# Hash-masked attention and a channel mix on one core: q and k of the third pair turned by TensorE, PSUM banks from a table, and another order of work

## The chip, the cores and the metric

One core of a Trainium2 chip. The metric is the time of one execution on the device, in microseconds (us). The engines are named as in the profile: PE (TensorE, with PEld for its weight loads), DVE (VectorE), ACT (ScalarE), POOL (GpSimd) and SP (SyncE, which here only issues DMAs).

## What is computed

Attention over 4 batches, 8 heads, 768 positions and 64 values a head, in which a query sees only keys of its own hash bucket, and behind it a channel mix with a squared ReLU and a gate:

```
bits(t)  = (t @ proj) > 0                      # 6 bits of each row of q and of k
scores   = q @ k.T / 8, where bits(q) == bits(k), else -1e9
x        = softmax(scores) @ v                 # (4, 768, 512), heads side by side
x_prev   = x one position later
xk, xr   = x_prev + mu * (x - x_prev)          # mu_k, mu_r
out      = sigmoid(xr @ w_r) * (relu(xk @ w_k) ** 2 @ w_v)
```

## The kernel before

The work goes by 16 pairs of heads (`n`), four pairs a batch, and after each fourth pair comes the batch's channel mix, called MoE in the code (`add_moe`).

For each pair, q and k are loaded in natural layout (`nat`, L481) and split in a high and a low half of 16 bits (`hi` L556, `lo` L559, into `nh`). They must then be turned, so that the 64 values and not the positions lie on partitions. For pairs 0 and 1 (`FIRSTS`) PE turns them (`add_prep_first`, L635; copied out of PSUM at L639), from the third pair on a DMA transpose does (`add_prep`, L563, on SP's queue). Of the turned tile `a`, rows 0 to 63 are the high half; over the low half, once it is used, the hash bits are written: PE takes the product with `proj` (L587 in `add_bits`), DVE keeps the sign (`bx`, L591), and DMAs on SP's queue send it to rows 64 to 69 of `a` (L599, called `row`). Pair 0 gets its bits without a DMA (L657, and L663 or L665). So the bits enter the score product itself, as rows of its contraction.

Scores come in nine steps of 1024 columns a pair (L708, `sc{n}_{s}`; steps 0 to 3 are of head 0 alone, 5 to 8 of head 1), each followed by an exp on ACT (L712). PV (L741, `oo`) gives the output and the sum of weights, DVE divides (L758), and the result is turned again (`ot` by PE for some pairs, by DMA L768 for the others), shifted by one position (`xs`, `xj`), and mixed (L829, L837, L841). `add_v` makes the values' 16 bit form and their sums (`va`, `vsum`). The MoE has `kp` (L859) with ReLU (L864 on ACT or L866 on DVE) and square (L869), `r` (L884) with a tanh (L887), and `v` (L896) with the last product (L903) and the store (L907). Weights are loaded in ten pieces (`wl`, L447) and cast (`wc`, L450 to L452).

Nothing of the order is left to a scheduler. Every operation is recorded with `add`; `ORDER` lists them all in the order in which they are issued, and each engine works through its own part of it, strictly in turn. `WHERE` says for each movable operation which engine does it. `Plan.schedule` in the old kernel walks through `ORDER` with planned times, only to choose a PSUM place for each operation that needs one: score steps take one of three pairs of banks (0 and 1, 2 and 3, 4 and 5), the others a single bank among 7 to 3. Three buffers of `vn` mean that the load of v for pair n + 3 waits for `va` of pair n; three of `nat` do the same for q and k.

Of the kernel before, what the change touches and what calls it, by code (L numbers as in the profile page):

```python
# [16 lines left out]

LAG = {"PE": 0.21, "ACT": 0.21, "DVE": 0.15, "POOL": 0.18, "SP": 1.8, "GQ": 2.0}
# [17 lines left out]
def R(kind, n):  # L36
# [4 lines left out]
    "wc0": "DVE", "wc1": "POOL", "wc2": "POOL", "wc3": "DVE", "wc4": "POOL", "wc5": "DVE", "wc6": "ACT", "wc7": "DVE",  # L41
    "wc8": "ACT", "wc9": "POOL", "hi0q0": "ACT", "evt0q00": "DVE", "evt0q01": "DVE", "hi0k0": "DVE", "evt0k00": "DVE", "beb0k00": "ACT",
    "evt0k01": "ACT", "beb0k01": "ACT", "hi0q1": "ACT", "evt0q10": "ACT", "hi0k1": "DVE", "evt0k10": "ACT", "beb0k10": "ACT", "va0": "POOL",
    "vsum0": "POOL", "vsum0b": "DVE", "vsum0c": "DVE", "hi1q0": "DVE", "evt1q00": "DVE", "hi1k0": "ACT", "evt1k00": "ACT", "hi1q1": "DVE",
    "evt1q10": "DVE", "hi1k1": "DVE", "evt1k10": "ACT", "xt0_0": "DVE", "xs0_0": "DVE", "xj0": "DVE", "va1": "POOL", "vsum1": "DVE",
    "vsum1b": "POOL", "vsum1c": "POOL", "hi2q": "DVE", "hi2k": "DVE", "xt1_0": "DVE", "xs1_0": "POOL", "xj1": "DVE", "va2": "POOL",
    "vsum2": "DVE", "vsum2b": "DVE", "vsum2c": "POOL", "hi3q": "DVE", "hi3k": "DVE", "xt2_0": "DVE", "xs2_0": "DVE", "xt2_3": "DVE",
    "xs2_3": "POOL", "xj2": "POOL", "va3": "POOL", "vsum3": "DVE", "vsum3b": "POOL", "vsum3c": "DVE", "hi4q": "DVE", "hi4k": "DVE",
    "xt3_0": "DVE", "xs3_0": "POOL", "xt3_3": "DVE", "xs3_3": "POOL", "xj3": "POOL", "relu0_0_0": "DVE", "relu0_0_1": "ACT", "relu0_1_0": "DVE",
    "relu0_1_1": "ACT", "relu0_2_0": "ACT", "relu0_2_1": "ACT", "relu0_3_0": "DVE", "relu0_3_1": "DVE", "relu0_4_0": "DVE", "relu0_4_1": "DVE", "relu0_5_0": "ACT",  # L50
    "relu0_5_1": "ACT", "relu0_6_0": "DVE", "relu0_6_1": "ACT", "relu0_7_0": "ACT", "relu0_7_1": "ACT", "va4": "POOL", "vsum4": "DVE", "vsum4b": "POOL",
    "vsum4c": "POOL", "hi5q": "DVE", "hi5k": "DVE", "xs4_0": "POOL", "va5": "DVE", "vsum5": "DVE", "vsum5b": "DVE", "vsum5c": "POOL",
    "hi6q": "DVE", "hi6k": "DVE", "xs5_0": "POOL", "va6": "DVE", "vsum6": "DVE", "vsum6b": "DVE", "vsum6c": "POOL", "hi7q": "DVE",
    "hi7k": "DVE", "xs6_0": "DVE", "va7": "POOL", "vsum7": "DVE", "vsum7b": "POOL", "vsum7c": "DVE", "hi8q": "DVE", "hi8k": "DVE",
    "xs7_0": "DVE", "relu1_0_0": "DVE", "relu1_0_1": "DVE", "relu1_1_0": "DVE", "relu1_1_1": "ACT", "relu1_2_0": "ACT", "relu1_2_1": "DVE", "relu1_3_0": "DVE",
    "relu1_3_1": "DVE", "relu1_4_0": "DVE", "relu1_4_1": "DVE", "relu1_5_0": "ACT", "relu1_5_1": "DVE", "relu1_6_0": "DVE", "relu1_6_1": "DVE", "relu1_7_0": "DVE",
    "relu1_7_1": "DVE", "vsum8": "DVE", "vsum8b": "DVE", "vsum8c": "DVE", "hi9q": "DVE", "hi9k": "DVE", "xs8_0": "POOL", "vsum9": "DVE",
    "vsum9b": "DVE", "vsum9c": "POOL", "hi10q": "DVE", "hi10k": "DVE", "xs9_0": "ACT", "vsum10": "DVE", "vsum10b": "DVE", "vsum10c": "DVE",
    "hi11q": "DVE", "hi11k": "ACT", "xs10_0": "DVE", "vsum11": "DVE", "vsum11b": "POOL", "vsum11c": "POOL", "hi12q": "ACT", "hi12k": "DVE",
    "xs11_0": "DVE", "relu2_0_0": "DVE", "relu2_0_1": "ACT", "relu2_1_0": "ACT", "relu2_1_1": "DVE", "relu2_2_0": "ACT", "relu2_2_1": "ACT", "relu2_3_0": "ACT",  # L60
    "relu2_3_1": "DVE", "relu2_4_0": "ACT", "relu2_4_1": "ACT", "relu2_5_0": "ACT", "relu2_5_1": "DVE", "relu2_6_0": "ACT", "relu2_6_1": "ACT", "relu2_7_0": "DVE",
    "relu2_7_1": "DVE", "vsum12": "DVE", "vsum12b": "POOL", "vsum12c": "POOL", "hi13q": "ACT", "hi13k": "ACT", "xs12_0": "DVE", "vsum13": "DVE",
    "vsum13b": "POOL", "vsum13c": "POOL", "hi14q": "DVE", "hi14k": "ACT", "xs13_0": "ACT", "vsum14": "DVE", "vsum14b": "DVE", "vsum14c": "DVE",
    "hi15q": "DVE", "hi15k": "ACT", "xs14_0": "POOL", "vsum15": "DVE", "vsum15b": "DVE", "vsum15c": "POOL", "xt15_0": "DVE", "xs15_0": "ACT",
    "relu3_0_0": "ACT", "relu3_0_1": "DVE", "relu3_1_0": "ACT", "relu3_1_1": "ACT", "relu3_2_0": "DVE", "relu3_2_1": "ACT", "relu3_3_0": "ACT", "relu3_3_1": "ACT",
    "relu3_4_0": "DVE", "relu3_4_1": "ACT", "relu3_5_0": "DVE", "relu3_5_1": "ACT", "relu3_6_0": "ACT", "relu3_6_1": "DVE", "relu3_7_0": "ACT", "relu3_7_1": "ACT",
# [3 lines left out]
ORDER = [  # L70
    31, 0, 2, 3, 1, 66, 63, 97, 98, 9, 35, 25, 4, 10, 5, 64, 6, 7, 8, 19, 71, 72, 65, 99,
    91, 77, 92, 81, 100, 14, 69, 73, 26, 82, 13, 78, 103, 93, 94, 87, 88, 74, 27, 28, 36, 122, 83, 84,
    123, 29, 30, 101, 95, 114, 115, 104, 68, 85, 41, 102, 89, 90, 167, 124, 168, 174, 175, 11, 75, 125, 96, 176,
    142, 146, 79, 15, 110, 177, 32, 111, 112, 118, 178, 86, 143, 147, 33, 293, 179, 144, 145, 80, 116, 67, 117, 119,
    140, 141, 120, 76, 113, 136, 137, 121, 134, 221, 228, 229, 222, 34, 126, 127, 129, 135, 132, 133, 39, 128, 138, 139,
    231, 232, 130, 131, 180, 181, 184, 185, 16, 192, 193, 186, 106, 107, 108, 109, 153, 187, 300, 301, 70, 170, 196, 197,
    105, 303, 148, 149, 150, 188, 189, 304, 151, 152, 198, 199, 183, 17, 171, 172, 182, 154, 155, 156, 40, 252, 224, 253,
    157, 244, 173, 230, 474, 475, 158, 245, 233, 18, 225, 240, 241, 226, 248, 249, 234, 235, 250, 251, 190, 191, 294, 477,
    478, 246, 247, 202, 194, 195, 159, 161, 467, 160, 203, 204, 205, 200, 201, 42, 206, 162, 165, 227, 266, 302, 223, 242,
    243, 166, 267, 268, 468, 207, 238, 528, 529, 269, 237, 208, 209, 239, 236, 324, 325, 270, 318, 305, 210, 211, 254, 37,  # L80
    38, 531, 470, 255, 306, 319, 307, 212, 213, 532, 214, 328, 271, 272, 273, 274, 316, 329, 317, 256, 257, 258, 476, 312,
    313, 169, 296, 479, 320, 321, 275, 215, 279, 47, 259, 260, 297, 298, 280, 281, 314, 261, 262, 315, 263, 326, 480, 264,
    265, 310, 322, 299, 471, 472, 163, 327, 323, 335, 336, 481, 337, 338, 164, 339, 308, 488, 489, 330, 331, 332, 333, 334,
    486, 522, 585, 276, 277, 521, 487, 311, 309, 498, 340, 582, 583, 499, 341, 342, 343, 344, 278, 490, 491, 502, 530, 345,
    346, 20, 347, 348, 349, 216, 503, 295, 494, 495, 492, 493, 219, 473, 504, 505, 485, 217, 350, 483, 550, 551, 533, 45,
    534, 496, 351, 497, 506, 586, 500, 501, 535, 484, 21, 283, 218, 284, 353, 354, 554, 555, 48, 524, 285, 525, 526, 352,
    22, 357, 482, 542, 282, 509, 510, 511, 512, 513, 507, 543, 508, 544, 545, 548, 549, 552, 553, 527, 584, 288, 289, 290,
    587, 588, 589, 540, 43, 355, 556, 557, 563, 564, 537, 539, 49, 538, 536, 541, 546, 46, 44, 547, 358, 359, 375, 565,
    356, 362, 363, 391, 50, 604, 605, 376, 364, 575, 602, 566, 567, 636, 637, 392, 377, 378, 371, 372, 606, 603, 607, 393,
    367, 368, 469, 373, 598, 369, 599, 578, 379, 380, 608, 381, 592, 609, 600, 601, 558, 559, 576, 639, 640, 610, 579, 580,  # L90
    611, 560, 561, 562, 581, 395, 396, 24, 382, 397, 220, 291, 398, 594, 595, 286, 287, 51, 590, 648, 53, 394, 593, 374,
    654, 292, 655, 649, 52, 630, 780, 781, 617, 618, 591, 660, 661, 411, 412, 638, 662, 619, 407, 408, 596, 663, 409, 370,
    413, 597, 641, 642, 643, 383, 384, 385, 664, 665, 629, 777, 778, 514, 515, 387, 652, 653, 388, 360, 389, 523, 632, 612,
    361, 365, 620, 621, 768, 650, 651, 410, 414, 55, 427, 366, 428, 429, 54, 658, 659, 403, 404, 613, 12, 614, 615, 399,
# [41 lines left out]
class Plan:  # L136
# [7 lines left out]
    def add(self, eng, dur, prio, fn, r=(), w=(), take=None, give=(), lag=None, name="", at=0.0, svc=0.0, off=None, tr=0, port=0, land=1.5):  # L144
# [31 lines left out]
        self.ops.append(o)  # L176
        return o

    def sequence(self):
        if ORDER:  # L180
            return [self.ops[i] for i in ORDER]
        left = {o.i: len(o.deps) for o in self.ops}
# [3 lines left out]
        while heap:  # L186
            o = self.ops[heapq.heappop(heap)[1]]
            seq.append(o)
            for s in o.succ:
                left[s] -= 1  # L190
                if not left[s]:
                    heapq.heappush(heap, (self.ops[s].prio, s))
# [772 lines left out]
```

## Time and profile before

| | |
|---|---|
| median of 3 runs | 249.64 us (249.36 to 250.64) |
| span of the profiled execution | 251.3 us |
| busy: PE, DVE, ACT, POOL | 236.9, 195.4, 179.1, 27.9 us |
| granted PE clock, mean | 0.983 |
| HBM read, written | 24.12 MB, 6.29 MB |

The profile is of one execution of its own, whose span is 1.7 us above the median; the page has no other time for it. In the rows, `x7` counts instructions that were merged, `SPq` is SP's queue of DMA issues, and the bracket at the end of a row of the timeline is the idle time before it and what ended it.

### The profile page before, as it was taken

How to read it: one execution, taken by the hardware profiler on the slowest of the kernel's cores; microseconds unless marked ns; L12 is line 12 of the kernel's file. 1: busy time of each engine (PE TensorE's matmuls, PEld its weight loads, DVE VectorE, ACT ScalarE, POOL GpSimd, SP SyncE). 2: the span in 40 equal slices, each digit the busy share in tenths (PEclk: the TensorE clock that was granted, in tenths of full speed). 3: DMA queues.
4: the chain of work that ended last, by engine and by line, in shares of the span. 5: the costliest groups of instructions: out<-in, count | busy, mean ns of one | idle time of the engine just before them, and what ended most of it. 6: DMA issues, size and time to landing. Idle time of an engine off the chain costs nothing.

```text
span 251.3 us, 6510 instructions
## 1 busy us (share of the span) xinstructions
PE 236.9 (94%) x2609; PEld 147.6 (59%) x2609; DVE 195.4 (78%) x471; ACT 179.1 (71%) x225; POOL 27.9 (11%) x73
## 2 busy tenths in 40 slices
PE   6886799999799998999999999999999999999993
PEld 2444578876566655666467566655865654545442
DVE  3795679889788889898998999899787878376322
ACT  5596689999799978996878899988787223332220
POOL 5002240541302031100001100100000000000000
PEclk9799799999999999999999999999999999999998
DMA  6999999999989999999999996793231030022223
GB/s 187 308 178 251 220 215 191 267 249 189 213 292 241 204 293 292 273 201 269 184 333 186 184 185 158 210 230 57 90 64 44 0 128 28 13 83 86 83 85 125
DMA packets 75194, 44.56 MB, mean 177 GB/s; under 512 B 55524, under 2 KB 70172, under 8 KB 75164
## 3 DMA queue, kind: packets, MB, share of 16 engines
q1 hardware_dynamic: 74028, 44.15, 72.8%
q8 instruction: 20, 0.33, 0.6%
q10 hardware_dynamic: 1136, 0.01, 0.3%
q14 instruction: 10, 0.08, 0.1%
HBM read 24.12 MB, written 6.29 MB: 121 GB/s over the span
## 4 chain that ended last, share of the span: by engine, by line
PE 75%; DMA 11%; DVE 8%; SPq 3%; ACT 1%; issue 1%; DVEq 0%
PE ps_all L708 19%; PE ps_all L896 17%; PE ps_all L859 13%; PE ps_all L741 12%; PE ps_all L884 8%; DMA nat<-in_k_dram 5%; PE ps_all L587 4%; DMA nat<-in_q_dram 3%; DMA a<-bx 2%; DMA os<-in_moe_w_k_dram 1%; DVE nh L559 1%; DVE nh L556 1%; PE ps_all L736 1%; ACT pt L712 1%; PE ps_all L794 1%
## 5 line engine op out<-in xcount | busy, mean ns | idle before, releaser
L712 ACT ACTIVATE pt<-ps_all 128x1024 bf16<-128x1024 f32 x144 | 138.8, 1040 | 21.1 <-PE ps_all L708 19.8
L708 PE MATMUL ps_all<-a 128*128 128x512 f16 (+3 forms) x408 | 80.6, 318 | 5.1 <-DMA a<-bx 3.9
L708 PEld LDWEIGHTS <-a 128*128 128x128 f16 x408 | 35.3, 98 | 26.7 <-DMA a<-bx 4.7
L859 PE MATMUL ps_all<-xk,wk 128*128 128x384 bf16 x256 | 49.0, 326 | 0.9 <-DVE kr L866 0.9
L896 PE MATMUL ps_all<-wv,k 128*128 128x512 bf16 (+1 forms) x200 | 45.9, 370 | 0.6 <-DVE os L903 0.6
L741 PEld LDWEIGHTS <-pt 128*128 128x128 bf16 x1152 | 42.1, 98 | 6.9 <-issue 1.1
L741 PE MATMUL ps_all<-va,pt 128*128 128x65 bf16 x1152 | 43.9, 194 | 0.0
L859 PEld LDWEIGHTS <-wk 128*128 128x128 bf16 x256 | 24.5, 98 | 17.6 <-issue 1.6
L896 PEld LDWEIGHTS <-k 128*128 128x128 bf16 x200 | 19.4, 98 | 20.6 <-issue 0.7
L864 ACT ACTIVATE kr<-ps_all 128x384 bf16<-128x384 f32 x33 | 15.8, 493 | 19.2 <-DVE k L869 12.7
L887 ACT ACTIVATE rs<-ps_all 128x512 f32<-128x512 f32 x24 | 14.2, 603 | 20.9 <-PE ps_all L884 19.0
L559 DVE SCALAR_TENSOR_TENSOR nh<-nat,nh 128x768 f16<-128x768 f32 x28 | 27.3, 976 | 1.1 <-ACT nh L554 0.6
L903 DVE SCALAR_TENSOR_TENSOR os<-rs,ps_all 128x512 f32<-128x512 f32 (+1 forms) x25 | 16.5, 662 | 14.7 <-PE ps_all L896 9.9
L869 DVE TENSOR_TENSOR k<-kr 128x384 bf16<-128x384 bf16 x64 | 21.5, 350 | 3.7 <-ACT kr L864 3.5
L884 PE MATMUL ps_all<-wr,xr 128*128 128x512 bf16 x96 | 23.8, 379 | 0.0
L866 DVE TENSOR_SCALAR kr<-ps_all 128x384 bf16<-128x384 f32 x31 | 17.1, 555 | 8.3 <-PE ps_all L859 6.6
L758 DVE TENSOR_TENSOR ob<-ps_all,rc 128x384 bf16<-128x384 f32 (+1 forms) x36 | 18.3, 511 | 1.0
L884 PEld LDWEIGHTS <-xr 128*128 128x128 bf16 x96 | 9.0, 98 | 10.0 <-ACT kr L864 0.3
L587 PE MATMUL ps_all<-a,p0g 128*32 128x256 f16 (+1 forms) x180 | 13.4, 276 | 1.3 <-DMA a<-nh 1.3
L556 DVE TENSOR_SCALAR nh<-nat 128x768 f16<-128x768 f32 x22 | 12.3, 557 | 3.0 <-DMA nat<-in_q_dram 2.5
L587 PE MATMUL ps_all<-a,p1g 128*32 128x256 f16 (+1 forms) x180 | 12.9, 273 | 0.0
L841 DVE TENSOR_TENSOR xr<-tm,xt 128x768 bf16<-128x768 f16 (+1 forms) x18 | 9.4, 520 | 0.4
(94 smaller groups left out, 187.4 us busy)
## 6 DMA issues: line engine op xcount, KB each, us to landing
vn<-in_v_dram SPq DMA_DIRECT2D x16, 384.0 KB
out_dram<-os SPq DMA_DIRECT2D x23, 256.0 KB
nat<-in_k_dram SPq DMA_DIRECT2D x15, 384.0 KB
nat<-in_q_dram SPq DMA_DIRECT2D x15, 384.0 KB
wst<-in_moe_w_k_dram SPq DMA_DIRECT2D x2, 512.0 KB
wst<-in_moe_w_r_dram SPq DMA_DIRECT2D x2, 512.0 KB
wst<-in_moe_w_v_dram SPq DMA_DIRECT2D x2, 512.0 KB
a<-bx SPq DMA_DIRECT2D x48, 9.0 KB
```

The lines of the kernel that those rows point to most:

```text
L559: nc.vector.scalar_tensor_tensor(out=nh[:, :, D:P], in0=nat.rearrange("p j (c d) -> p (j c) d", d=D), scalar=QS, in1=nh[:, :, 0:D], op0=AL ...
L587: nc.tensor.matmul(ps[g_ * wid : (g_ + 1) * wid, 0:FW], w_[:, m_ - 1 - x : m_ - 1 - x + wid], a_t[sa][:, i, x % NFOLD * FW : (x % NFOLD + ...
L708: nc.tensor.matmul(ps[:, lo - s * STEP : hi - s * STEP], side_a["k"][sa][:, j, jc * P : (jc + 1) * P], side_a["q"][sa][:, j, q0 : q0 + hi ...
L712: nc.scalar.activation(out=pt_t[sp][:, s * STEP : (s + 1) * STEP], in_=ps_t[plan.slot[nm]], func=AF.Exp, bias=EBIAS, scale=ESC)
L741: nc.tensor.matmul(oo[:, (ic - c0) * 65 : (ic - c0) * 65 + 65], pt_t[sp][:, o : o + P], va_t[sa][:, j, jc, 0 : D + 1], start=(not uc and i ...
L758: nc.vector.tensor_tensor(out=ob_t[so][:, c0:c1, j * D : (j + 1) * D], in0=oo[:, :, 0:D], in1=rc_t[sr][:, 1, c0:c1].unsqueeze(2).to_broadc ...
L859: nc.tensor.matmul(ps[:, 0:HALF], wk_sb[:, d, fc * P : (fc + 1) * P], xk_t[mx[d]][:, h * HALF : (h + 1) * HALF], start=(d == 0), stop=(d = ...
L866: nc.vector.tensor_scalar(out=kr_t[sk], in0=sm(nm)[:, 0:HALF], scalar1=0.5 ** 0.5, scalar2=0.0, op0=ALU.mult, op1=ALU.max)
L869: nc.vector.tensor_tensor(out=k2_t[s2][:, h * HALF : (h + 1) * HALF], in0=kr_t[sk], in1=kr_t[sk], op=ALU.mult)
L884: nc.tensor.matmul(sm(nr), xr_t[mx[d]][:, c * P : (c + 1) * P], wr_sb[:, d, :], start=(d == 0), stop=(d == NDC - 1))
L896: nc.tensor.matmul(sm(nv)[:, lo:hi], k2_t[(b * NFC + fc) % NK2][:, c * P : (c + 1) * P], wv_sb[:, fc, lo:hi], start=(fc == 0), stop=(fc == ...
L903: nc.vector.scalar_tensor_tensor(out=os_t[so][:, lo:hi], in0=rs_t[s1][:, lo:hi], scalar=1.0, in1=sm(nv)[:, lo:hi], op0=ALU.add, op1=ALU.mult)
```

## The change

The third pair joins `FIRSTS`, so its q and k are converted head by head and turned by PE, 24 transposes in four groups and four copies out of PSUM, and two DMA transposes are gone. The loads of the first pair and all that follows from them take head 1 first. PSUM places are no longer chosen by planned times: the table `SLOT` names a bank (or the first of two) for every operation, among the same classes. `mu_k` and `mu_r` are loaded as eight rows of 128 and turned by a small matmul with an 8 x 8 identity, in place of two loads with one value on each partition and step. `WHERE` and `ORDER` are new throughout: they were sought for an order that also holds when GpSimd's operations take up to twice their planned time. More is done on GpSimd: 37 of 48 sums of v (18 before), 9 of 10 casts of weights (4), six conversions of q or k (none), 10 of 18 shifts (8); ReLU is on DVE 36 times (31) and on ACT 28 (33). Other things that the new code can do are switched off (`NWARM2 = 0`, `ROWD = ()`, `ROW_ACT = ()`, `STEPS = {}`).

```diff
-    FIRSTS = (0, 1)
+    FIRSTS = (0, 1, 2)
...
     def schedule(self):
-        free = {e: 0.0 for e in ("PE", "ACT", "DVE", "POOL", "SP")}
...
+        used, held = set(), {}
+        order = [self.ops[i] for i in ORDER]
         for o in order:
...
+                name, size = o.take[1], BANKS[o.take[0]]
+                self.slot[name] = SLOT[name]
+                held[name] = set(range(SLOT[name], SLOT[name] + size))
...
-    for t, src, key in ((muk, moe_mu_k, "muk"), (mur, moe_mu_r, "mur")):
...
+    add("POOL", 0.3, -2.2, lambda: make_identity(nc, id8), w=["id8"], name="id8")
+    for i_, src in enumerate((moe_mu_k, moe_mu_r)):
+        add("ACT", 0.42, -19.0, lambda i_=i_, src=src: nc.scalar.dma_start(out=mu8[i_ * NDC : (i_ + 1) * NDC, :], in_=src.rearrange("(c p) -> c p", p=P)),
...
+    add("PE", 0.12, 1.0, lambda: nc.tensor.matmul(sm("mu")[:, 0 : 2 * NDC], mu8, id8, start=True, stop=True),
```

The start of the order, engine by engine (the digits behind q or k are pair, then head):

```
before  DVE  hi0k1 lo0k1 lo0q0 lo0q1 hi0k0 lo0k0 evt0q01 evt0q00 hi1k1 evt0k00 lo1k1 lo1k0 hi2 lo2
             beb0q10 hi1q0 hi2 lo1q0 hi1q1 lo2 beb0q01 lo1q1 beb0q00 evt1q00 evt1q10 hi3 lo3 bx1
after   DVE  hi0k1 lo0k1 hi0q1 lo0q1 evt0k10 hi0k0 evt0q10 lo0k0 lo0q0 beb0q10 hi1k1 lo1k1 hi1q1 evt0k01
             lo1q1 beb0q01 lo1q0 lo1k0 beb0q00 beb0k01 evt1k00 evt1k10 evt1q00 hi2k1 hi2k0 lo2q0 lo2q1 bx1
before  SP   q, k of pairs 0, 1, 2, 3, 5q, 4; tr2 tr2 and ldv0 among them; row1 row1 ldv1 ldv2 row2 row2 tr3 tr3 ...
after   SP   q, k of pairs 0, 1, 2, 3, 4; ldv0 ldv1 ldv2 ldv3 among them; row1 row1 5k 5q ldv4 6q row2 row2 tr3 tr3 tr4 tr4
             6k 7q row3 row3 ldv6 wl2 ldv5 row4 row4 8q row4 row4 tr5 tr5 tr6 tr6 ...
after   POOL ... hi1k0 ... hi2q0 va0 ... va1 ... vsum0 vsum0b vsum0c ... hi4 id8 vsum1 ...
```

The last matmuls before are the second half of columns of `v3_5`, stored by itself; after, all columns of `v3_4`.

## The prediction

> **What bounds the kernel now.** I read the page first, for the share of each engine, then windows of the span, PE's waits, the chain that ended last, and the timeline of the first 25 us.
>
> ```profile
> span 251.3 us, 6510 instructions
> PE 236.9 (94%) x2609; PEld 147.6 (59%) x2609; DVE 195.4 (78%) x471; ACT 179.1 (71%) x225; POOL 27.9 (11%) x73
> ```
>
> TensorE (PE) is the busiest engine, 236.9 of 251.3 us, so a better order can win at most the 14.4 us in which it is idle, and whatever it loses to a low clock. The windows say where both lie (columns: busy us of PE, PEld, DVE, ACT, POOL, then granted clock, DMA share, GB/s):
>
> ```profile
> 20.00:25.00 5.00, 2.72 (x31) 1.72 (x29) 2.27 (x4) 2.98 (x4) 1.32 (x2) 1.00 0.84 262
> 25.00:30.00 5.00, 3.37 (x24) 2.04 (x25) 3.95 (x6) 2.73 (x3) 1.43 (x3) 0.77 1.07 228
> 30.00:35.00 5.00, 4.99 (x84) 3.90 (x83) 2.63 (x8) 3.74 (x5) 1.69 (x3) 0.89 0.95 254
> 65.00:70.00 5.00, 3.66 (x61) 2.38 (x60) 3.53 (x11) 3.63 (x5) 1.04 (x2) 1.00 0.85 267
> 90.00:100.00 10.00, 8.99 (x108) 5.28 (x110) 8.74 (x23) 7.20 (x10) 1.15 (x5) 1.00 1.13 272
> 100.00:160.00 60.00, 60.00 (x727) 37.68 (x717) 54.56 (x132) 50.77 (x61) 4.39 (x9) 1.00 0.99 223
> 160.00:240.00 80.00, 80.00 (x697) 46.16 (x696) 58.44 (x150) 43.28 (x64) 0.81 (x2) 1.00 0.29 80
> ```
>
> From 100 to 240 us PE is never idle: there a change of engine or of order wins nothing, it can only lose. Between 20 and 30 PE is idle 3.9 us, and the clock is low from then to about 31. Around 65 and 95 another 1.3 and 1.0 us are missing. PE's waits and the chain that ended last name the causes:
>
> ```profile
> PE ps_all L708 <- DMA a<-bx: 3.9, 1, 3.9
> PE ps_all L587 <- DMA a<-nh: 1.3, 2, 1.0
> ...
> 22.07 4.43 DMA a<-bx
> 26.63 1.70 PE ps_all L708 x7
> ```
>
> The second pair's scores (L708) start at 26.63, when its hash bits, sent from `bx` to rows 64 to 69 of `a`, have landed. That transfer is what the start ends on, so I ask when `bx1` comes about now, and when in the new order.
>
> **The change part by part.** From the timeline, the start, with the instructions that I price with:
>
> ```profile
> 0.96 0.59 ACTq L404 DMA_DIRECT2D pj<-in_proj_dram  x1
> 3.19 0.36 DVE L618 TENSOR_SCALAR nh<-nat 128x384 f16<-128x384 f32 x1 [2.07 <-DMA nat<-in_k_dram]
> 3.42 0.24 POOL L405 TENSOR_SCALAR npj<-pj 64x6 f32<-64x6 f32 x1 [1.83 <-DMA pj<-in_proj_dram]
> 9.39 0.35 DVE L639 COPY a<-ps_all 128x384 f16<-128x384 f16 x1
> 9.66 1.02 DVE L621 SCALAR_TENSOR_TENSOR nh<-nat,nh 128x384 f16<-128x384 f32 x2
> 10.59 0.56 DVE L556 TENSOR_SCALAR nh<-nat 128x768 f16<-128x768 f32 x1
> 11.18 0.96 DVE L559 SCALAR_TENSOR_TENSOR nh<-nat,nh 128x768 f16<-128x768 f32 x1
> 12.17 1.55 SPq L563 DMA_TRANSPOSE a<-nh  x1
> 12.17 0.95 DVE L665 TENSOR_SCALAR a<-ps_all 6x768 uint16<-6x768 uint16 x1
> 13.81 2.86 ACT L712 ACTIVATE pt<-ps_all 128x1024 bf16<-128x1024 f32 x3 [0.60 <-PE ps_all L708]
> 15.62 2.04 SPq L563 DMA_TRANSPOSE a<-nh  x1
> 15.62 0.56 DVE L665 TENSOR_SCALAR a<-ps_all 6x384 uint16<-6x384 uint16 x1
> 16.82 0.51 PE L635 MATMUL ps_all<-idh,nh 128*128 128x128 f16 x6 [0.43 <-DVE nh L621]
> 17.38 1.02 DVE L639 COPY a<-ps_all 128x768 f16<-128x768 f16 x2
> 20.00 0.42 DVE L591 TENSOR_SCALAR bx<-ps_all 128x256 uint16<-128x256 uint16 x1
> 20.45 2.36 SPq L599 DMA_DIRECT2D a<-bx  x2
> ```
>
> *When the first exps start.* VectorE (DVE) works through a fixed order from 3.19 on. Before, the bits of head 1's q (L665, 6x768) stand behind 14 instructions, among them a conversion and a rest (L556, L559; 0.56 + 0.96) for the third pair, and start at 12.17. In the new order head 1 comes first: they stand behind three of L618 (0.36), four of L621 (0.51) and two copies of 768 (0.51), 4.1 us, so at about 7.6 with half a us of waits. In ScalarE's queue eight short instructions stand ahead of the first exp, one of them a conversion of the third pair's q, which DVE had at 10.59 before; I put the first exp at 10.3, an estimate, against 13.81. That is not yet the gain: nine exps of about 0.95 (2.86 for three) then reach to 19, and only the next pair's rows let the queue go on.
>
> *When `bx1` is ready.* Now 27 instructions of DVE stand before L591: five of L618, eight of L621, three each of L556 and L559, three copies of 384 (0.35), two of 768, one L665 of 0.95 and two of 0.56: 1.8 + 4.1 + 1.7 + 2.9 + 1.1 + 1.0 + 2.1 = 14.7 us. From 3.19 that is 17.9, and it stands at 20.00, so 2.1 us are waits. After, again 27: seven of L618, ten of L621, none of the long ones, one copy of 384, five of 768, the 0.95 and three of 0.56: 2.5 + 5.1 + 0.35 + 2.55 + 0.95 + 1.7 = 13.2, so 16.4 without waits and 18.5 with as many. I take 17.6, and 18.0 at its end (bounds 16.8 and 18.9).
>
> *The rows' flight.* Before, 26.63 - 20.42 = 6.2 us passed from `bx1` to PE, behind loads issued just ahead. The nearest row of a lone small transfer is pj: issued at 0.96, used at 3.42, 2.5 us; with the first of two issues ahead of it (half of 2.36) 3.7. In the new order SP's queue reaches the rows early, its last load ahead being the fourth v. So 3.7 to 6.2; I take 4.4, between, nearer the lone one. The second pair's scores then start at 22.4 against 26.63: **4.2 us gained**; with both bounds 1.5 to 6.1.
>
> *The clock.* Windows 25 to 35 lose (0.23 + 0.11) x 5 = 1.7 us of full clock, right after the long wait. With `bits1`, `bits2` and the new transposes ahead, PE's wait would be about 2 us. I count **1.7 us gained**; if the wait stays long, nothing. The Trainium skill, "TensorE: Matmul & The Clock Gate", section "What's actually happening", says that the clock goes to half after an idle window of about 3.4 us; the wait of 3.9 us with 0.77 behind it agrees, and by it a 2 us wait leaves the clock full.
>
> *The third pair turned by PE.* It removes two DMA transposes (1.55 + 2.04 us of SP's queue, and their DMA), and adds 24 transposes on PE (four of the 0.51 row, 2.0 us) and four copies out of PSUM; the conversions are the same columns in halves. The 2.0 us lie among the first pair's last scores, which wait for exps, in the stretch where PE is now idle 2.3 us (window 20 to 25); without that cover they cost 2.0 in full. Behind them `bits2` stays as it is.
>
> *What SP's queue holds after the rows.* Four loads of v go ahead of the first rows, against one before. The fourth waits for `va0` on GpSimd, which stands behind `hi1k0` and `hi2q0`; queued behind it on SP are the rows of pairs 1 and 2 and every later transpose. From the timeline of SP:
>
> ```profile
> 30.68 0.46 SPq L481 DMA_DIRECT2D nat<-in_q_dram  x1
> 37.83 1.57 SPq L599 DMA_DIRECT2D a<-bx  x2
> 39.45 3.54 SPq L563 DMA_TRANSPOSE a<-nh  x2
> 55.59 2.50 SPq L563 DMA_TRANSPOSE a<-nh  x1
> ```
>
> and from the groups by form (mean ns after the comma):
>
> ```profile
> L501 POOL CAST va<-vn 128x768 bf16<-128x768 f32 x6 | 5.6, 930 | 25.6 <-DMA vn<-in_v_dram 19.3 <-PE ps_all L741 6.1 <-PE ps_all L859 0.2
> L509 POOL TENSOR_TENSOR vt<-va 128x390 f32<-128x390 bf16 x1 | 0.8, 847 | 0.1
> L450 POOL CAST wk<-k 128x1024 bf16<-128x1024 f32 x1 | 1.4, 1450 | 0.0
> L903 DVE SCALAR_TENSOR_TENSOR os<-rs,ps_all 128x512 f32<-128x512 f32 x23 | 15.6, 683 | 13.4 <-PE ps_all L896 8.5 <-ACT rs L887 2.8 <-ACT kr L864 1.1
> L903 DVE SCALAR_TENSOR_TENSOR os<-rs,ps_all 128x256 f32<-128x256 f32 x2 | 0.8, 421 | 1.4 <-PE ps_all L896 1.4
> ```
>
> No row shows a conversion to halves on GpSimd. Its bounds are the cast of as many columns (0.93 for 768) and the two-input add scaled by columns (0.847 x 768 / 390 = 1.7); for 384 half of each. With the second pair's k there by 9, two of at most 0.85 and `va0` are done by 11.7, five us before `bx1`: hidden. [...] The new order also takes up `bits5` later among the scores, so I expect short waits for transposes or rows, 0 to 3 us more than now: **1.3 lost**.
>
> *The rest.* `mu` in eight rows, turned by one small matmul, and one VectorE instruction in place of two: between 0.3 lost and 0.3 gained, hidden before the first mix; I count 0. Banks from a table: still two or three score buffers of two banks each, no instruction more; 0. GpSimd gets 103 listed operations for 67, VectorE 439 for 455, ScalarE 215 for 227; from 100 us on PE has no idle time that this could fill: 0, at worst the rival below. The end: the last step becomes a whole row block in place of a half, 0.68 for 0.42 us on VectorE and a store of twice the size: **0.5 lost** (0.3 to 0.9).
>
> **Sum.** The profiled execution's span is 251.3, 1.7 above the median of 249.64; the difference is carried over. -4.2 - 1.7 + 1.3 + 0.5 = -4.1: **245.5 us** by the median.
>
> **The rivals.** *Given back to the queue.* If loads and transposes set the pace up to 100 us (DMA share 0.84 to 1.13 in every window above), PE comes early and waits: the gain shrinks to the 3.6 us of two transposes less the loads that newly stand ahead of the first rows, three of v for one of q, two in net, of 384 KB at the 262 GB/s of the window from 20 on, 1.5 us each: 249.0. For it: L587 waits for `a<-nh` 1.3 us, in the window at 65. [...]
>
> *More than forecast.* With rows at the lower bound (-6.1), the clock, and the 1.3 at 65 gone, no new wait: 249.64 - 6.1 - 1.7 - 1.3 + 0.5 = 241.0.
>
> *GpSimd late, slower than before.* Nine of ten weight casts go to GpSimd, as do most v sums, six conversions and the shifts of x. Before the first MoE matmuls (L859) its queue holds, in this order, `hi8`, v sums, `wc1`, `wc0`, `wc3`, `wc4`; L859 waits in PE's queue, and scores and PV of the next pairs wait behind it. Casts took 1.0 to 1.45 us. If they take twice 1.2 or more beside VectorE, five of them are 6 us late, and the sums and shifts behind them another us: 245.5 + 7 = 252.5. It decides from about twice the time that rows show; below that, the queue's slack hides it. For it: a kind of contention is in the rows, 1450 against 1040 for equal casts:
>
> ```profile
> L450 POOL CAST wk<-wst 128x1024 bf16<-128x1024 f32 x1 | 1.0, 1040 | 0.0
> ```
>
> Against: even doubled, GpSimd's 28 us plus about 35 more stay under half the span. The Trainium skill, "SBUF — State Buffer", section "SBUF: two separate sides", speaks against the change: GpSimd and certain VectorE instructions hold a shared pair of ports exclusively, and the other blocks; the 1450 agrees in direction, and by it what moves to GpSimd also slows VectorE.
>
> **How the numbers follow.** The forecast with its bounds 0.52, more than forecast 0.14, given back 0.12, GpSimd late 0.22. What a measurement can tell from no change is 0.5%, 1.2 us. Faster than 248.4: the first two and a little of the third, 0.68; within 0.5%: 0.10; slower: 0.22. The range runs from the better rival to half way into the slow one, 241.0 to 251.5, and leaves out about 0.2.
>
> **What would show it.** Right: the first exp near 10.3, the second pair's first L708 near 22.4, no clock below 1 in the windows from 15 to 40, PE full from 25 on. Wrong: L708 or L587 waiting for `a<-bx` or `a<-nh` for over 3 us in total up to 100 us (given back); L859, L741 or L736 waiting for POOL, or VectorE's L559 and L829 for POOL, with casts over 2.4 us (GpSimd late); or any PE idle time after 100 us, which the forecast takes as none.

## The result, and the profile after

The changed kernel takes 257.6 us (median of four, 256.98 to 259.18) against 250.14: ratio 1.031 (95% interval 1.026 to 1.037). In two later sets it was 256.12 against 250.44, ratio 1.021 (1.014 to 1.028), and 256.04 against 250.23, ratio 1.032 (1.025 to 1.039). The ratios count fast runs alone, which in the last set leaves five of the eleven runs of the kernel before, 246.36 to 249.75 us. The forecast was 245.5, the range 241.0 to 251.5. From the page, and the same windows as before:

```profile
span 255.2 us, 6584 instructions
PE 237.7 (93%) x2635; PEld 147.9 (58%) x2635; DVE 195.0 (76%) x455; ACT 172.2 (67%) x213; POOL 66.3 (26%) x110
```

```profile
20.00:25.00 5.00, 4.99 (x61) 3.53 (x59) 4.85 (x9) 4.02 (x5) 3.74 (x5) 1.00 0.68 212
25.00:30.00 5.00, 4.48 (x77) 3.24 (x75) 2.80 (x4) 5.00 (x7) 0.00 (x0) 1.00 1.27 232
30.00:35.00 5.00, 4.53 (x51) 3.21 (x49) 3.17 (x9) 4.55 (x6) 1.28 (x3) 1.00 1.04 180
65.00:70.00 5.00, 4.90 (x91) 4.04 (x92) 4.64 (x10) 4.86 (x6) 3.13 (x3) 1.00 1.42 223
90.00:100.00 10.00, 9.78 (x157) 6.59 (x156) 7.13 (x22) 8.26 (x10) 2.56 (x5) 1.00 0.99 195
100.00:160.00 60.00, 57.38 (x688) 35.71 (x686) 49.55 (x115) 50.76 (x62) 18.99 (x21) 1.00 0.91 216
160.00:240.00 80.00, 80.00 (x666) 45.47 (x663) 58.44 (x148) 34.29 (x54) 5.22 (x11) 1.00 0.22 67
```

The start came as forecast up to 25: PE is full from 20 on and the clock is whole. It doesn't stay full, as the forecast had it: from 25 to 35 it is busy 9.01 of 10 us, and from 40 to 60 18.06 of 20 us, where before it was busy all 20. From 100 to 160, where PE had no idle time, 2.62 us of it are idle now, and GpSimd is busy 18.99 us there, not 4.39. VectorE has 16 instructions fewer and is as long busy. The exps, of the changed kernel and then of the one before:

```profile
11.54 2.89 ACT L707 ACTIVATE pt<-ps_all 128x1024 bf16<-128x1024 f32 x3
23.54 2.85 ACT L707 ACTIVATE pt<-ps_all 128x1024 bf16<-128x1024 f32 x3 [0.54 <-PE ps_all L703]
```

```profile
27.27 1.94 ACT L712 ACTIVATE pt<-ps_all 128x1024 bf16<-128x1024 f32 x2 [3.95 <-PE ps_all L708]
```

The tenth exp, the second pair's first, starts at 23.54 and not at 27.27: 3.7 us ahead. Part of what takes that back is seen best at one place, in the timeline of the changed kernel:

```profile
108.83 2.84 POOL L433 CAST wv<-wst 128x1024 bf16<-128x1024 f32 x2
108.99 1.78 DVE L542 SCALAR_TENSOR_TENSOR nh<-nat,nh 128x768 f16<-128x768 f32 x1
...
113.39 1.11 POOL L492 TENSOR_TENSOR vt<-vn 128x384 f32<-128x384 f32 x1 [1.03 <-DMA vn<-in_v_dram]
113.57 1.14 DVE L864 TENSOR_TENSOR k<-kr 128x384 bf16<-128x384 bf16 x1
...
114.77 0.61 PE L891 MATMUL ps_all<-wv,k 128*128 128x512 bf16 x2 [1.02 <-DVE k L864]
```

The square L864 needs 0.35 us. Here it starts 0.18 after a GpSimd sum and ends 0.2 after it, and PE waits 1.02 us for it. Counted over the trace, 27 VectorE instructions take over 0.15 us more than their form does elsewhere, 12.9 us in all, each beside a GpSimd instruction that started earlier; before there were 4, of 2.0 us. No wait of PE's matmuls, of VectorE or of ScalarE ends on a GpSimd result here; on SP's queue 2.7 us of waits do. GpSimd's own rows (mean ns of one after the comma):

```profile
L539 POOL TENSOR_SCALAR nh<-nat 128x768 f16<-128x768 f32 x4 | 8.9, 2224 | 12.7 <-DMA a<-bx 6.2 <-PE ps_all L630 3.6 <-DMA a<-nh 2.8
L492 POOL TENSOR_TENSOR vt<-vn 128x384 f32<-128x384 f32 x7 | 7.4, 1053 | 40.1 <-DMA vn<-in_v_dram 36.1 <-DVE vs L498 4.0
L495 POOL TENSOR_TENSOR vt<-vt 128x128 f32<-128x128 f32 x7 | 4.6, 651 | 9.2 <-DVE vt L492 8.8
```

The conversion takes 2.22 us, above the bounds of 0.93 and 1.7, and L495 takes 0.651 where its row before had 0.414. PE's longest waits in the stretch behind the start, and at the end:

```profile
PE ps_all L570 <- DMA a<-nh: 1.9, 4, 0.9
PE ps_all L891 <- DVE os L898: 1.6, 1, 1.6
PE ps_all L731 <- DVE ob L753: 1.2, 3, 0.6
...
PE ps_all L891 <- DVE k L864: 1.0, 1, 1.0
PE ps_all L703 <- DMA a<-bx: 0.8, 1, 0.8
```

The end, in the timeline:

```profile
245.23 0.69 DVE L898 SCALAR_TENSOR_TENSOR os<-rs,ps_all 128x512 f32<-128x512 f32 x1 [0.98 <-PE ps_all L891]
248.07 0.42 DVE L898 SCALAR_TENSOR_TENSOR os<-rs,ps_all 128x256 f32<-128x256 f32 x1 [2.16 <-DMA out_dram<-os]
...
251.40 0.69 DVE L898 SCALAR_TENSOR_TENSOR os<-rs,ps_all 128x512 f32<-128x512 f32 x1 [1.36 <-PE ps_all L891]
```

VectorE waits 2.16 us for an output buffer whose store stands late in SP's queue, and PE 1.6 us for VectorE.

PE's idle time can be added up over the two profiles. Up to 40 us it falls from 8.1 to 5.3 us; from 40 to 100 it grows from 2.6 to 4.1, from 100 to 160 from 0 to 2.6, and from 240 on from 3.8 to 5.5. With 0.9 us more of PE's own work that makes the 3.9 us by which the spans differ.

### The profile page after: what moved, and what is told of

The parts are those of the page before. It is cut to its first block, busy times and chain, and to the rows that moved or that the text cites. A ratio compares the mean times of both kernels' runs of the same rounds, so it can differ in the third digit from the quotient of the medians.

```text
span 255.2 us, 6584 instructions
## 1 busy us (share of the span) xinstructions
PE 237.7 (93%) x2635; PEld 147.9 (58%) x2635; DVE 195.0 (76%) x455; ACT 172.2 (67%) x213; POOL 66.3 (26%) x110
## 4 chain that ended last, share of the span: by engine, by line
PE 61%; DVE 17%; DMA 14%; issue 4%; SPq 1%; ACT 1%; DVEq 0%
PE ps_all L891 15%; PE ps_all L854 14%; PE ps_all L703 13%; DMA a<-nh 7%; PE ps_all L736 7%; PE ps_all L879 6%; PE ps_all L570 4%; DVE nh L542 3%; DVE nh L539 2%; DVE ob L753 2%; DMA nat<-in_q_dram 2%; DMA xt<-ob 2%; DVE k L864 1%; DVE nh L616 1%; DVE os L898 1%
## 5 line engine op out<-in xcount | busy, mean ns | idle before, releaser
L703 PE MATMUL ps_all<-a 128*128 128x256 f16 (+3 forms) x408 | 80.0, 316 | 1.7 <-DMA a<-bx 0.8
L736 PEld LDWEIGHTS <-pt 128*128 128x128 bf16 x1152 | 43.3, 97 | 8.9 <-issue 1.8
L703 PEld LDWEIGHTS <-a 128*128 128x128 f16 x408 | 34.5, 97 | 21.5 <-issue 4.2
L736 PE MATMUL ps_all<-va,pt 128*128 128x65 bf16 x1152 | 45.5, 193 | 0.0
L864 DVE TENSOR_TENSOR k<-kr 128x384 bf16<-128x384 bf16 x64 | 23.7, 385 | 6.5 <-ACT kr L859 3.9
L859 ACT ACTIVATE kr<-ps_all 128x384 bf16<-128x384 f32 x28 | 13.4, 491 | 15.5 <-PE ps_all L854 14.1
L861 DVE TENSOR_SCALAR kr<-ps_all 128x384 bf16<-128x384 f32 x36 | 19.7, 553 | 4.6 <-PE ps_all L854 3.9
L492 POOL TENSOR_TENSOR vt<-vn 128x384 f32<-128x384 f32 x7 | 7.4, 1053 | 40.1 <-DMA vn<-in_v_dram 36.1
L570 PE MATMUL ps_all<-a,p0g 128*32 128x256 f16 (+1 forms) x180 | 14.1, 276 | 2.4 <-DMA a<-nh 1.9
L539 DVE TENSOR_SCALAR nh<-nat 128x768 f16<-128x768 f32 x20 | 13.4, 674 | 0.5 <-DMA a<-nh 0.5
L836 DVE TENSOR_TENSOR xr<-tm,xt 128x768 bf16<-128x768 f16 (+1 forms) x18 | 11.6, 647 | 2.7 <-PE ps_all L879 2.7
```

Of the source, the lines that this page charges most:

```text
L570: nc.tensor.matmul(ps[g_ * wid : (g_ + 1) * wid, 0:FW], w_[:, m_ - 1 - x : m_ - 1 - x + wid], a_t[sa][:, i, x % NFOLD * FW : (x % NFOLD + ...
L703: nc.tensor.matmul(ps[:, lo - s * w : hi - s * w], side_a["k"][sa][:, j, jc * P : (jc + 1) * P], side_a["q"][sa][:, j, q0 : q0 + hi - lo], ...
L736: nc.tensor.matmul(oo[:, (ic - c0) * 65 : (ic - c0) * 65 + 65], pt_t[sp][:, o : o + P], va_t[sa][:, j, jc, 0 : D + 1], start=(not uc and i ...
L861: nc.vector.tensor_scalar(out=kr_t[sk], in0=sm(nm)[:, 0:HALF], scalar1=0.5 ** 0.5, scalar2=0.0, op0=ALU.mult, op1=ALU.max)
L864: nc.vector.tensor_tensor(out=k2_t[s2][:, h * HALF : (h + 1) * HALF], in0=kr_t[sk], in1=kr_t[sk], op=ALU.mult)
```

## Experiments

Theory: GpSimd's larger share holds VectorE up. Rivals: the order itself; the end; the transposes.

**A second profile of the kernel before** (no edit).

> The kernel before, unchanged, for a second profile of it. If its first profile (span 251.3 us) held an unusually long wait at the start, this one has a span of 247.5 to 249.5 us, and the first scores of the second pair start earlier than the 26.63 us of the first profile, by about as much as the span is shorter. If the time above the median lay in the middle or is spread, that start stays within 0.5 us of 26.6 us.

252.43 us, span 250.6, tenth exp at 26.7, 0.6 earlier, behind a wait of 3.1 us in place of 3.9: the long wait at the start is no accident of one profile. In all runs here the time of an execution is its span plus 1.7 to 2.1 us, 1.8 in this one.

**Engines alone, both ways.** `before_where_after` has the `WHERE` of the change, the rest as before; `after_where_before` the reverse.

```diff
-    "wc0": "DVE", ... "vsum1": "DVE", ... "hi4k": "DVE", ...
+    "wc0": "POOL", ... "vsum1": "POOL", ... "hi4k": "POOL", ...
```

> The kernel before with its order, transposes and PSUM banks kept, and only the engines as in the changed kernel (38 us more on GpSimd). Theory GpSimd: 253 to 257 us, over 20 lengthened VectorE instructions. Rival order: 249.5 to 251 us, since the sequence that is blamed is not in it.

> The changed kernel with its order, banks and transposes kept, but each conversion, sum and copy of input on the engine on which the kernel before had it (the two new ones, second-head q of pair 2 and k of pair 1, on VectorE and ScalarE). Theory GpSimd (work moved to GpSimd lengthens VectorE's instructions and arrives late): the lengthened VectorE instructions fall from 27 to under 10, TensorE's idle time between 25 and 120 us falls, and the time is 251 to 253.5 us. Rival order (the new sequence itself is worse): 256 to 259 us, with the idle stretches where they are now. A gain of 1 to 3 us says that both have part.

The first: 255.25 us, ratio 1.028 (1.019 to 1.037), 19 lengthened instructions (over 20 expected) with 10.4 us. So 5.9 us of loss come with the engines alone. But not all of that is hold-up. VectorE also waits 5.7 us for two conversions on GpSimd, and PE 2.2 us for its sums, the longest of them in the second row:

```profile
DVE nh L564 <- POOL nh L561: 5.7, 2, 3.3
...
PE ps_all L741 <- POOL vsu L520: 1.4, 1, 1.4
```

The second went the other way than expected: 264.69, ratio 1.064 (1.057 to 1.072), though only 9 instructions (4.0 us) are lengthened. Its timeline tells why:

```profile
162.71 0.56 DVE L492 TENSOR_TENSOR vt<-vn 128x384 f32<-128x384 f32 x1 [4.52 <-DMA vn<-in_v_dram]
...
163.60 0.56 DVE L753 TENSOR_TENSOR ob<-ps_all,rc 128x384 bf16<-128x384 f32 x1
...
164.21 0.97 PE L854 MATMUL ps_all<-xk,wk 128*128 128x384 bf16 x5 [2.71 <-DVE ob L753]
```

In this order the v sums stand where GpSimd can wait for their load (36.1 us of waits in its L492 row). Put back on VectorE, such a sum stops VectorE's whole queue for 4.52 us, and PE 2.71. Order and engines belong together: neither can be priced in the other's surroundings.

**Is it the running instruction?** GpSimd additions that nobody reads, put into the kernel before.

```diff
+            nc.gpsimd.tensor_tensor(out=scr, in0=scr, in1=scr, op=ALU.add)   # 128 x 192, fp16
```

> The kernel before with its order, engines and PSUM banks kept, and 96 GpSimd additions on a scratch tile of 192 columns that nobody reads, two behind each GpSimd step from the first v copy on; at 0.45 to 0.6 us each they are 43 to 58 us of GpSimd time. No result waits for them except through GpSimd's own queue (at most about 1.1 us). Theory GpSimd in the form that a running GpSimd instruction holds VectorE up: over 15 VectorE instructions are lengthened by more than 0.15 us each and the time is 251.5 to 255 us. If only late GpSimd results cost time and not the running instruction: no more lengthened instructions than the 4 of the kernel before, and 249.8 to 251.2 us.

> The kernel before with order, engines and PSUM banks kept, and 102 GpSimd additions on a scratch tile that nobody reads, now only behind those GpSimd steps after which the profile of before shows GpSimd idle for 2 us or more, and never more than fill that gap, so that hardly any real GpSimd step waits for them. At 0.49 us each (as in the kernel with adds behind each step) they are 50 us of GpSimd time, as there. Theory hold-up (a running GpSimd instruction holds VectorE up): 15 to 40 lengthened VectorE instructions, and 252 to 260 us. Rival queue (the adds cost time only by standing ahead of real GpSimd steps): 249 to 251 us, however many VectorE instructions are lengthened. Between 251 and 252 us both have part, with the greater share for the queue.

Behind each step: 262.18 us, ratio 1.052 (1.043 to 1.062), 7 us more than the theory's upper end, 40 lengthened instructions, 12.2 us. In gaps only: 257.91, ratio 1.035 (1.028 to 1.041), 45 of them, 13.9 us. They took 0.64 us each and not 0.49 (0.62 behind each step), so the gaps were filled more than meant. Still 7.8 of 12.8 us remain, and little of that is lateness: VectorE waits 3.5 us for GpSimd's results, 2.2 before, and PE never. PE's waits for VectorE grow from 5.7 to 10.5 us. The hold-up is most of the 7.8. Groups of the kernel with gap adds, then of the one before:

```profile
L875 DVE TENSOR_TENSOR k<-kr 128x384 bf16<-128x384 bf16 x64 | 26.2, 423 | 3.5 <-ACT kr L870 3.3
L565 DVE SCALAR_TENSOR_TENSOR nh<-nat,nh 128x768 f16<-128x768 f32 x28 | 29.6, 1058 | 1.1 <-ACT nh L560 0.6
L764 DVE TENSOR_TENSOR ob<-ps_all,rc 128x384 bf16<-128x384 f32 x28 | 15.5, 555 | 0.7
L942 POOL TENSOR_TENSOR scr<-scr 128x192 f16<-128x192 f16 x102 | 65.3, 640 | 6.7
```

```profile
L869 DVE TENSOR_TENSOR k<-kr 128x384 bf16<-128x384 bf16 x64 | 21.5, 350 | 3.7 <-ACT kr L864 3.5
L559 DVE SCALAR_TENSOR_TENSOR nh<-nat,nh 128x768 f16<-128x768 f32 x28 | 27.3, 976 | 1.1 <-ACT nh L554 0.6
L758 DVE TENSOR_TENSOR ob<-ps_all,rc 128x384 bf16<-128x384 f32 x28 | 15.5, 555 | 0.7
```

**Which moves?** Five conversions alone, or all the others, in the order before.

```diff
+    "hi1k0": "POOL", "hi4k": "POOL", "hi8q": "POOL", "hi12q": "POOL", "hi14k": "POOL"     # before_hi_pool; all but these: before_rest_pool
```

> The kernel before with order, transposes and PSUM banks kept, and only the five conversions that the changed kernel has on GpSimd moved there (k of pair 1's first head, k of pair 4, q of pairs 8 and 12, k of pair 14): 9 to 11 us more on GpSimd. Theory long instructions (the 2.2 us conversions hold VectorE up and come late): 252 to 254 us, more than half of the 5.9 us that all moves together cost. Rival sum of small ones: 249.5 to 251 us, and the rest of the moves carries the cost.

> The kernel before with order, transposes and PSUM banks kept, and all moves between engines of the changed kernel except those five conversions: weight casts, v copies and sums, copies of the layer's input, some 28 us more on GpSimd. Theory long instructions: 250 to 252 us. Rival sum of small ones: 253 to 255.5 us, close to the 255.25 us of all moves together.

251.91 us, ratio 1.010 (1.006 to 1.015), and 253.89, 1.015 (1.006 to 1.024): 1.8 and 3.8 us, together 5.5, close to the 5.9, though the two intervals overlap. The two differ in kind, as a row of the conversions alone shows, and then one of all the others:

```profile
L564 DVE SCALAR_TENSOR_TENSOR nh<-nat,nh 128x768 f16<-128x768 f32 x28 | 26.8, 958 | 6.4 <-POOL nh L561 5.4
```

```profile
L874 DVE TENSOR_TENSOR k<-kr 128x384 bf16<-128x384 bf16 x64 | 23.7, 385 | 3.5 <-ACT kr L869 3.3
```

With the conversions on GpSimd only 2 VectorE instructions are lengthened (958 ns against 976 before), but VectorE waits 5.4 us for converted halves. With the short moves 19 are lengthened, by some 10 us in all (385 ns against 350), and VectorE waits for GpSimd nowhere. So in the order before the conversions cost by late results, and the short moves mostly by hold-up.

**The end.** Stores right behind their products (those of `v2_3` and `v2_4` too), `v3_4` ahead of the halves of `v3_5`.

```diff
-    ... os3_0 st3_0 st2_5 ... os3_1 ... os3_3 ... os3_2 ... st3_3 st3_1 st3_2 ... v3_5 st3_5 v3_4 st3_4
+    ... os2_5 st2_5 ... os3_0 st3_0 os3_1 st3_1 os3_3 st3_3 os3_2 st3_2 v3_4 st3_4 v3_5 st3_5
```

> The changed kernel with only its end put as in the kernel before: each store of the last layer blocks issued right behind its product, and the whole block 3_4 ahead of the two halves of block 3_5 rather than behind them. Theory tail (1.6 us of TensorE idle for an output buffer whose store is queued late, and a whole block's product and store at the very end): the idle 1.62 us before the last products goes, and the time falls by 1.5 to 2.5 us to 255 to 256 us. Rival (the end is bound by TensorE's work whatever the order): within 0.7 us of 257.6 us.

253.65 us, ratio 1.018 (1.011 to 1.025): more than expected, but 3.3 of the 5.0 us between the two spans were there at the last exp, up to which nothing in the order differs. The changed kernel again, and then both as a pair:

> The changed kernel unchanged, on the same chip as the three others of this set, for a second profile. Its end should show TensorE idle for about 1.6 us ahead of the last products again, and its time should be 256.5 to 258.5 us. If instead it comes out at 254 to 256 us, part of the 4 us that the repaired end seemed to give belongs to the spread between sets of runs.

> The changed kernel unchanged, as the other half of a pair on one chip with the next run. Its eight times so far run from 254.85 to 259.18 us; 256 to 258 us are expected here.

> The changed kernel with the repaired end, on the same chip as the run before. Theory end: the end alone is worth the 1.6 us of idle time and the 0.6 us by which the last store ended later, so 1.6 to 2.4 us less than its partner. Rival whole 4 us: 3.3 to 4.5 us less, which would mean that the order of the last stores also changes what happens before 240 us. Rival spread: less than 1 us less.

256.12 (ratio 1.021), with the 1.6 us of idle time at its end again; then 256.04 against 253.80 (ratios to before 1.032, 1.025 to 1.039, and 1.022, 1.012 to 1.032). The end is worth about 2.2 us, though the intervals overlap; the rest of the 4 is spread between sets.

**In the changed kernel's own order,** with the repaired end: the six conversions off GpSimd; or wide GpSimd steps in thirds and quarters.

```diff
-    "hi1k0": "POOL", "hi2q0": "POOL", "hi4k": "POOL", "hi8q": "POOL", "hi12q": "POOL", "hi14k": "POOL"
+    "hi1k0": "ACT", "hi2q0": "DVE", "hi4k": "DVE", "hi8q": "DVE", "hi12q": "ACT", "hi14k": "ACT"      # after_tail_hi
...
-            e.tensor_tensor(out=vt[:, :, :, 0:E], in0=src[:, :, 0:3, 0:E], in1=src[:, :, 3:6, 0:E], op=ALU.add)
+            for x in range(3) if e is nc.gpsimd else ():                                              # after_tail_split
+                e.tensor_tensor(out=vt[:, :, x, 0:E], in0=src[:, :, x, 0:E], in1=src[:, :, x + 3, 0:E], op=ALU.add)
```

> The changed kernel with the repaired end, and besides the six conversions of q and k that it has on GpSimd put on VectorE (three) and ScalarE (three). In the order of the kernel before five of them cost 1.8 us. Theory GpSimd: 251 to 253 us, the lengthened VectorE instructions at 15 to 20 of 27. Rival (this order was laid out for its own engines, as the return of all placements at once, 264.7 us, suggests): 254 to 257 us.

> The changed kernel with the repaired end, and each wide GpSimd step (conversions, v copies, first v sum, weight casts) issued as three or four instructions of a third or a quarter of the columns; same engines, same order. Theory hold-up (VectorE waits for the GpSimd instruction that runs when it starts): no wait can exceed a short instruction's 0.3 to 0.6 us, the surplus in lengthened VectorE instructions falls from 12.4 us to under 8 us, and the time falls by 1 to 3 us from 253.65 us, to 251 to 252.7 us. Rival (GpSimd's results come late, whoever is held up): GpSimd becomes 3 to 6 us busier by the added instructions, and the time stays at 253.5 to 256 us.

255.62 and 255.59 us (1.018, 1.010 to 1.025, and 1.019, 1.010 to 1.027), where the repaired end alone had 1.018 and 1.022. Neither gained. Without conversions on GpSimd some 25 instructions are still lengthened, not 15 to 20. Shorter instructions did cut the surplus from 12.4 to 6.9 us, but GpSimd was busy 94 us, not 66, and a cast that came late let PE wait 2.35 us near 111. Hold-up seems to have been traded for lateness. So in this order no run shows what the hold-up costs.

**The start.** In the kernel before: pair 1's bits first; or pair 2 turned by PE; then the changed start, up to pair 3's first sums, ahead of the old order and engines.

```diff
-    hi2 lo2 tr2 ... hi3 lo3 ... bits1 bx1 row1 row1           # before_bx1_first
+    ... bits1 bx1 hi2 lo2 hi3 lo3 row1 row1 tr2
...
-    FIRSTS = (0, 1)                                           # before_t2_pe
+    FIRSTS = (0, 1, 2)
-    hi2 lo2 tr2 hi2 lo2 tr2 ... sc0_1 sc0_4
+    hi2 lo2 hi2 lo2 ... sc0_1 t2q (two, each with its evt2) sc0_4 t2k (two, each with its evt2)
...
+    ORDER = first 271 steps of the changed order, then the rest in the old order; WHERE as before   # hybrid
```

> The kernel before with one move at the start and nothing else: VectorE's conversions for pair 3 (first half) and for the k side of pair 2, with its transpose on the SP queue, are issued behind the sign bits of pair 1 and the copies of their rows, no longer ahead of them. Theory start (pair 1's scores wait for these rows 3.9 us in the profile of before, and three VectorE microseconds stand ahead of them): the wait falls by 2 to 3.5 us and the time by 1.5 to 3 us, to 247 to 248.6 us. Rival given back (what starts earlier waits later, as pair 2's transposes and pair 1's v sums come later): 249.5 to 251 us.

> The kernel before with one part of the change alone: q and k of pair 2 turned by TensorE and copied out of PSUM by VectorE, in place of the two transposes on the SP queue; conversions at the same places in VectorE's order, the eight new steps ahead of the last scores of pair 0. TensorE gets 2.0 us more work there and VectorE some 2 to 3 us more, ahead of pair 1's first scores or beside them. Theory cost: 251 to 253 us. Rival (the SP queue is freed by 3.6 us of transposes, so the rows of pair 1 land earlier): 248 to 250 us.

> The start of the changed kernel (its steps up to pair 3's first sums, q and k of pair 2 turned by TensorE, second head first) and behind it the order and the engines of the kernel before, GpSimd's share and the end included; PSUM banks drawn anew. Theory: the start is worth 3 to 5.6 us, TensorE's extra work costs 2.0 us, and nothing else of the change remains: 246.5 to 249.5 us, first scores of the second pair at 23 to 24.5 us. Rival (a lead at the start is lost again in whatever follows, because the later work waits for VectorE and for loads and not for TensorE): 249.8 to 253 us with the early start still in the trace.

254.29 us (1.017, 1.009 to 1.025): the rows left at 19.62 and not at 20.45, but PE then waited 4.5 us for the transpose that had been pushed back:

```profile
PE ps_all L592 <- DMA a<-nh: 7.0, 5, 4.5
```

254.45 (1.015, 1.008 to 1.021): PE is busy 5.71 of the 6 us from 20, so the wait is gone, and yet the tenth exp comes at 27.6, no earlier; the first comes at 15.54, 1.4 to 1.7 us later than in the two profiles of before. 255.78 (1.025, 1.017 to 1.032): its second pair's scores start at 24.9, not 23 to 24.5, its tenth exp at 25.5, and by the 37th it is at 53.9 us where the kernel before is at 53.7. Hybrid, then the second profile of before:

```profile
40.00:100.00 60.00, 53.44 (x760) 37.16 (x758) 50.23 (x124) 51.73 (x61) 10.47 (x20) 1.00 0.91 199
```

```profile
40.00:100.00 60.00, 57.95 (x861) 40.75 (x859) 52.41 (x133) 55.80 (x67) 13.49 (x26) 1.00 1.05 241
```

4.5 us of PE work are missing from that stretch. PE's waits, all of these between 40 and 100, say what for:

```profile
PE ps_all L673 <- DMA a<-bx: 2.9, 3, 1.9
PE ps_all L824 <- DVE kr L831: 1.8, 2, 1.4
...
PE ps_all L540 <- DMA a<-nh: 1.1, 1, 1.1
```

That is 4.0 us for rows and transposes from SP's queue, against 0.9 there in the second profile of before, and 1.8 for `kr` against 0.9. So the lead was given back to the queue, mostly. A lead at the start is not by itself a gain at the end. Why the rows land late stays open: the hybrid's PSUM banks were drawn anew, and two orders meet in it.

## Why the prediction was wrong

*First exps, bits, rows: right.* First exp 11.54 against 10.3 forecast, `bx1` at 18.21 against 17.6, 4.3 us from its end to PE against 4.4, and a lead of 3.7 at the second pair's first exp against 4.2 (3.2 against the second profile of before). *The clock: right* in the profile, 1.00 in every window shown. But seven other runs of the kernel before were granted 0.984 to 1.000 on the mean, where its profile has 0.983: the 1.7 us were not lost in each of them.

*The third pair turned by PE: open.* The step said that the 2.0 us lie under waits for exps. Alone, in the order before, they gave 254.45 for 250.44, with no lead at the tenth exp, so there they aren't free. In the changed kernel the lead came with them in place, and no run prices them there.

*The queue: right in size.* No run shows the 1.3 us by itself. Behind the start L570 waited 1.9 us for `a<-nh` and L703 0.8 for `a<-bx` (at 159), 2.7 together, where before it was 1.3: 1.4 more.

*GpSimd at 0: the step that failed.* I priced it by when its results come, against its own idle time, and took PE's full stage from 100 us on as safe. In the order before the engines alone cost 5.9 us, with GpSimd busy a quarter of the span: some 1.8 by conversions that come late and 3.8 by short moves that lengthen VectorE's instructions. In the changed kernel no engine but SP waits long for GpSimd, while 27 VectorE instructions are lengthened; the hold-up's share of the loss there is argued from that and not measured, as neither experiment in its own order gained. The rival "GpSimd late" had the right sign, but for this kernel the wrong mechanism and the wrong point: it was to decide from twice the time of the rows, with L859 waiting for casts as its sign. Casts took 1.04 to 1.77 us, and no such wait is there. The rule of the Trainium skill, "SBUF — State Buffer", section "SBUF: two separate sides", stood in the text as a direction and got no term in the sum.

*"From 100 us on no idle time": read the wrong way.* It excluded a gain and I booked 0. A stage in which PE is full and VectorE busy 54.56 of 60 us has room only to lose; 2.62 us of PE idle time came there.

*The end: mis-sized,* 0.5 forecast, 2.2 measured, with intervals that overlap. I priced the larger block and not the stores: they come in another order, and with them the output buffers.

*The reference point.* Span plus 1.8 us is the time, so the profile of before, 251.3, stood for 253.1: 3.5 above the median that I subtracted from, not 1.7.

Added up, -3.7 (the lead, PE's extra work within it) + 5.9 + 2.2 = +4.4, against 5.7 to 7.5 measured. The 5.9 were measured in another order and hold late conversions that the changed kernel doesn't wait for, so the sum need not close. Between the two profiles PE's idle time does account for the 3.9 us. The rest is that the profiled execution of before took 3.0 us more than the median of 250.14 and that of the changed kernel 0.6 less than its own; why stays open. No version had a lower median than the kernel before.

## What to carry to other kernels

Work moved to an idle engine is priced twice: by when its result comes, and by what it does to the engine beside it while it runs. The two can be told apart in a trace: waits that end on the idle engine for the one, the neighbour's instructions whose duration grows, form by form, for the other. An order written out by hand fits its engines: moving either alone can cost more than both together, and a lead at the start can be given back to a queue further on.

## What the runs showed of the hardware

In the kernel with gap adds, of the VectorE instructions that began while a GpSimd one had 0.05 us or more to run, the square (k from kr) was lengthened 13 times in 17 and the rest (nh from nat and nh) 9 in 12, while those that read PSUM never were: `kr` 0 of 11, `ob` 0 of 9, `bx` 0 of 7. The group rows above agree: 350 to 423 and 976 to 1058 ns, `ob` 555 in both. The Trainium skill, "SBUF — State Buffer", section "SBUF: two separate sides", puts it so: VectorE instructions with two SBUF inputs, or in a mode that uses two ports, and GpSimd share a pair of ports that whichever starts first keeps for its whole instruction. The trace agrees, in the ends too: the 1.14 us square above ends 0.2 us after the GpSimd sum, somewhat under the 0.35 that it needs alone. GpSimd pays as well, 0.651 for 0.414 us in the small sum.
